# A written order for VectorE and ScalarE around the join of two MLPs

## The chip, the cores and the metric

One core of a Trainium2 chip runs the whole kernel in one launch. The metric is the device time in microseconds. TensorE (PE) multiplies, VectorE (DVE) and ScalarE (ACT) do the elementwise work, SyncE (SP) issues nearly all DMAs, GpSimd is hardly used. Each engine takes its own instructions in their order and waits on semaphores for the others.

## The reference

```python
# q, k, v: (4, 8, 576, 64)
attn = softmax(mask(q @ k.T / sqrt(64))) @ v   # heads 0-3: 32 keys back; heads 4-7: every 32nd key
x = attn.transpose(0, 2, 1, 3).reshape(2304, 512)
h = x @ moe_w_in                     # 512 -> 2048
x = maximum(h, 0)**2 @ moe_w_out     # 2048 -> 512
h = x @ moe2_w_in
out = (h * sigmoid(1.702 * h)) @ moe2_w_out
```

The weights of both MLPs come as 64-bit floats. The kernel's matmuls take 32-bit operands of reduced precision, so each operand is split into a high part and a low remainder, and a product is three matmuls: high by high, low by high, high by low.

## The kernel before

**Weights** are fetched as pairs of 32-bit words and turned into 32-bit floats by five steps (`decode_ops`, lines 138 to 158): ScalarE takes the absolute value of the upper word (L142), VectorE clamps, shifts, and joins the two words (L144, L146, L151, L155). A cast on ScalarE then makes the high part, a subtraction on VectorE the low part.

**The first MLP** runs over five blocks of tokens (512, 512, 256, 512, 512) and, in each, over 16 slices f of the hidden dimension. For a slice TensorE does 12 matmuls into a bank "h" (L412), `act_sq` makes the square and its halves (L441 Relu on ScalarE, L442 high half gh on ScalarE, L443 the square on VectorE, L444 low half gl on VectorE), and while it does so TensorE runs the 12 second-layer matmuls of the slice before (`second`, L469: eight with gh, then four with gl). The attention of later blocks is done beside the earlier ones.

**Preparing the second MLP** happens beside the first MLP's blocks 3 and 4 (counted from 0). `PLAN` (L758) says before which slice what is recorded: "d" converts two slices of the second MLP's first-layer weights (`decode2(0, p)`), forms the seven sums that a Strassen-like scheme needs (L585), splits them into wst (L588, L589) and writes them to w2d in DRAM (L590); "e" converts two slices of its second-layer weights (`decode2(1, p)`, halves whl, L581 and L582); "m" is `make_x`, the sums of the input and their halves xop (L619, L620, L623); "s" streams the products' weights back (L644, L648). Only TensorE's order is the written one here (L727). VectorE's, ScalarE's and SyncE's order is chosen by a scheduler when the program is built, from what is recorded; `issue_after` (L141) keeps a conversion's first step behind a marked instruction of `act_sq`.

**The second MLP** makes three passes over 768 tokens. A pass has two halves of 384 tokens: in the first, eight pairs of slices (f = 2p and 2p + 1) are done as seven products of six matmuls each (`product`, L655) in place of eight; partial results go to X (bank "att"), Y and Z (bank "h"), and are copied and added on ScalarE and VectorE into s1, s2, s3 (L842 to L869). s1 and product 5 give this half's two values per pair, s2 and s3 the other half's, which are kept in gst. Sigmoid and product are `act_sig` (L449, L452), the halves gh and gl `split_g` (L457, L458). Nine second-layer matmuls per slice (`mm_acc2`, L487) follow: six with gh, three with gl. They run one pair later, after products 1 and 4. At the end of the first half the last pair's 18 matmuls are done token tile by token tile with their stores, then the second half does its 16 slices from gst, 9 matmuls each, with `make_x` for the next pass, one operation per slice, between them.

Of the kernel before, what the change touches and what calls it, by code (L numbers as in the profile page):

```python
# [21 lines left out]
def kernel(  # L22
# [88 lines left out]
    marks = [None, None]  # L111
# [26 lines left out]
    def decode_ops(s, t1, mark):  # L138
        low, high = s[:, :, 0], s[:, :, 1]
        ti = t1.bitcast(I32)  # L140
        with tc.issue_after(mark.ins) if mark else ExitStack():  # L141
            nc.scalar.activation(t1, high.bitcast(F32), AF.Abs)  # L142
        yield
# [16 lines left out]
    def decode(n, pool, ntmp):  # L160
# [10 lines left out]
        yield from decode_ops(s.rearrange("p (n two) -> p n two", two=2), t, None)  # L171
# [266 lines left out]
    def act_sq(ph, i):  # L438
        nb = BLOCKS[i][1]
        t, gh, gl = act_tiles(nb)  # L440
        marks[0] = nc.scalar.activation(t, ph[:, 0:nb], AF.Relu)  # L441
        marks[1] = nc.scalar.activation(gh, t, AF.Square)  # L442
        nc.vector.tensor_tensor(out=t, in0=t, in1=t, op=ALU.mult)  # L443
        nc.vector.tensor_tensor(out=gl, in0=t, in1=f32(gh), op=ALU.subtract)  # L444
        return gh, gl

    def act_sig(h, g):
        t, = act_tiles(NH, ("t",))
        marks[0] = nc.scalar.activation(t, h, AF.Sigmoid, scale=1.702)  # L449
        if g is None:  # L450
            g = t
        nc.vector.tensor_tensor(out=g, in0=h, in1=t, op=ALU.mult)  # L452
        return g

    def split_g(g):
        gh, gl = act_tiles(NH, ("gh", "gl"))
        marks[1] = nc.scalar.copy(gh, g)  # L457
        nc.vector.tensor_tensor(out=gl, in0=g, in1=f32(gh), op=ALU.subtract)  # L458
        return gh, gl
# [98 lines left out]
    raw = {}  # L558

    def fetch2(o, p, s):  # L560
        raw[o, p] = s
        for x in range(2):
            fetch_raw(s[:, x], (w2_in, w2_out)[o], 2 * p + x, o)

    def decode2(o, p):
        s, t = raw.pop((o, p)), tmp()
        t2 = t[:, 0:4].rearrange("p (x y) n -> p x (y n)", x=2)
        for x in range(2):
            for _ in decode_ops(s[:, x].bitcast(I32).rearrange("p (n two) -> p n two", two=2), t2[:, x], marks[x]):
                pass  # L570
        if o:
            for x in range(2):
# [3 lines left out]
                elif x == 0:  # L576
                    w2 = slot(f, [2, 2, DM], F32R, "whl")
# [19 lines left out]
    def slot(f, shape, dt, name):  # L597
# [3 lines left out]
        return wpools[n >= NF // 2].tile([P, *shape], dt, tag="w", name=name, bufs=NF // 2 - (FS if n < NF // 2 else 0))  # L601
# [9 lines left out]
    def make_x(s):  # L611
# [5 lines left out]
        def split(j, x):  # L617
            h, l = xops[j][:, 0:2], xops[j][:, 2:4]
            nc.scalar.copy(h, x)  # L619
            nc.vector.tensor_tensor(out=l, in0=x, in1=f32(h), op=ALU.subtract)  # L620

        def sub(out, a, b):
            nc.vector.tensor_tensor(out=out, in0=a, in1=b, op=ALU.subtract)  # L623

        if not wbuf:
            for _ in range(7):
                t_ = slot(0, [2048], F32R, "xop")
                xops.append(t_[:, 0:4 * NH].rearrange("p (h n) -> p h n", h=4))
                wbuf.append(t_[:, 4 * NH:2048].rearrange("p (h n) -> p h n", h=2))
        for fn, args in (  # L630
# [3 lines left out]
            fn(*args)  # L634
            yield
# [92 lines left out]
    stage, xraw = None, None  # L728

    def prepare(what):  # L730

        nonlocal stage, xraw
        for kind, n in what:
            if kind == "stage":
                stage = ring(2, [2, DM], I64, "stage")
            elif kind == "stages":
                stage = ring(1, [2, 2, DM], I64, "stage")
            elif kind in "io":
                fetch2("io".index(kind), n, stage)
            elif kind == "f":  # L740
                fetch2(1, n, stage[:, n % 2])
            elif kind == "d":
                decode2(0, n)
            elif kind == "e":
                decode2(1, n)
            elif kind == "t":

                d = lpool.tile([P, 1], F32, tag="one", name="one", bufs=1)
                nc.scalar.activation(d, f32(gs[4, 0][0][:, 0:1]), AF.Sigmoid)
            elif kind == "x":  # L750
                xraw = load_raw(0, 0)
            elif kind == "m":
                for _ in make_x(xraw):
                    pass
            elif kind == "s":
                stream(n)

    PLAN = {  # L758
# [4 lines left out]
    }  # L763

    for i in range(1, N1):
        for f in range(NF):
# [3 lines left out]
            prepare(PLAN.get((i, f), ()))  # L770
# [26 lines left out]
            gs[i, f] = act_sq(ph, i)  # L797
# [159 lines left out]
```

## Time and profile before

| what | value |
|---|---|
| median of 3 runs (lowest, highest) | 900.73 us (900.62, 901.32) |
| profiled execution, own time | 900.57 us |
| its span, first to last instruction | 898.8 us |
| TensorE busy | 878.7 us, 98% of the span, 5203 matmuls |
| VectorE busy | 553.9 us, 62% |
| ScalarE busy | 447.0 us, 50% |
| granted TensorE clock | 1.00 in all slices |
| DMA, mean rate | 137 GB/s |

The span leaves out some 1.8 us before the first and after the last instruction. Busy shares are means over stages: an engine at 62% can be full for 20 us. Matmuls overlap and their ends are modelled, so the start of one matmul to the start of a later one is what can be measured.

### The profile page before, as it was taken

The numbers are of one execution on the slowest core, as the hardware profiler recorded it, in microseconds if no ns is written. First come the engines' busy times: TensorE is split into PE (matmuls) and PEld (weight loads), VectorE is DVE, ScalarE is ACT, GpSimd is POOL, SyncE is SP. The second block draws the span as 40 slices with busy tenths as digits, with TensorE's granted clock in tenths as the row PEclk, the third lists the DMA queues.
The fourth block names the chain that finished last, engine by engine and source line by source line (L and its number), as shares of the span: only waits on it lengthen the run. The fifth ranks groups of instructions, "written<-read, shape, count | busy, mean of one in ns | idle before, by whom it ended". The sixth has DMA issues, their size and how long they took to land.

```text
span 898.8 us, 14141 instructions
## 1 busy us (share of the span) xinstructions
PE 878.7 (98%) x5203; PEld 749.3 (83%) x5209; DVE 553.9 (62%) x1362; ACT 447.0 (50%) x1153; POOL 2.6 (0%) x12
## 2 busy tenths in 40 slices
PE   8999999999999999999989999999999999999998
PEld 5678887888889998888868899987899978999986
DVE  5999995544546544877797688755344473444432
ACT  7888886453545543445444365543333352333322
POOL 0000000000000000000000000000000000000000
PEclk9999999999999999999999999999999999999999
DMA  8996210221103220556866386553344430344200
GB/s 204 304 334 204 63 27 26 86 53 35 43 20 112 46 71 1 175 202 215 299 233 234 139 276 249 195 184 117 115 163 158 163 129 1 117 164 164 82 36 35
DMA packets 96088, 122.99 MB, mean 137 GB/s; under 512 B 37812, under 2 KB 83604, under 8 KB 93460
## 3 DMA queue, kind: packets, MB, share of 16 engines
q1 hardware_dynamic: 95876, 121.97, 41.5%
q8 instruction: 41, 0.67, 0.3%
q14 instruction: 27, 0.22, 0.1%
q10 hardware_dynamic: 144, 0.13, 0.0%
HBM read 97.96 MB, written 24.12 MB: 136 GB/s over the span
## 4 chain that ended last, share of the span: by engine, by line
PE 79%; DVE 12%; DMA 3%; ACT 3%; issue 2%; SPq 1%; DVEq 0%; ACTq 0%
PE ps_acc L487 21%; PE ps_h L412 17%; PE ps_acc L469 16%; PE ps_att L655 11%; PE ps_h L655 8%; PE ps_att L285 2%; DVE tmp L151 1%; PE ps_h L364 1%; DVE tmp L155 1%; DMA w2d<-wst 1%; PE ps_att L264 1%; PE ps_att L339 1%; DVE whl L181 1%; DVE tmp L144 1%; DVE xop L620 1%
## 5 line engine op out<-in xcount | busy, mean ns | idle before, releaser
L412 PE MATMUL ps_h<-xr,whl 128*128 128x512 f32 (+1 forms) x948 | 211.0, 371 | 0.8 <-DVE whl L181 0.8
L412 PEld LDWEIGHTS ps_h<-xr,whl 128*128 128x128 f32 x948 | 164.4, 188 | 32.0 <-DVE whl L181 1.3
L487 PE MATMUL ps_acc<-whl,gh 128*128 128x512 f32 x576 | 149.1, 392 | 2.6 <-ACT gh L457 2.6
L469 PE MATMUL ps_acc<-gh,whl 128*128 128x512 f32 (+1 forms) x640 | 148.6, 374 | 0.0
L487 PEld LDWEIGHTS ps_acc<-whl,gh 128*128 128x128 f32 x576 | 106.9, 188 | 24.1 <-ACT gh L457 5.1
L469 PEld LDWEIGHTS ps_acc<-gh,whl 128*128 128x128 f32 x640 | 110.3, 188 | 19.1
L315 ACT ACTIVATE pr<-pr,st 72x72 f32<-72x72 f32 (+1 forms) x224 | 81.1, 367 | 20.4 <-DVE st L301 20.4
L441 ACT ACTIVATE t<-ps_h 128x512 f32<-128x512 f32 (+1 forms) x64 | 34.6, 540 | 113.5 <-PE ps_h L412 97.9
L487 PE MATMUL ps_acc<-whl,gl 128*128 128x512 f32 x288 | 82.6, 392 | 2.0 <-DVE gl L458 1.8
L469 PE MATMUL ps_acc<-gl,whl 128*128 128x512 f32 (+1 forms) x320 | 79.0, 369 | 3.7 <-DVE gl L444 3.7
L469 PEld LDWEIGHTS ps_acc<-gl,whl 128*128 128x128 f32 x320 | 56.7, 188 | 14.5 <-DVE gl L444 4.5
L487 PEld LDWEIGHTS ps_acc<-whl,gl 128*128 128x128 f32 x288 | 53.9, 188 | 15.3 <-DVE gl L458 3.8
L443 DVE TENSOR_TENSOR t<-t 128x512 f32<-128x512 f32 (+1 forms) x64 | 39.8, 622 | 34.5 <-ACT gh L442 33.9
L655 PE MATMUL ps_att<-xop 128*128 128x384 f32 x288 | 58.4, 337 | 1.1 <-ACT hs L842 1.1
L449 ACT ACTIVATE t<-hs 128x384 f32<-128x384 f32 x72 | 37.9, 526 | 41.5 <-DVE gst L452 33.5
L655 PE MATMUL ps_att<-xop,wst 128*128 128x384 f32 x288 | 58.5, 338 | 0.0
L655 PEld LDWEIGHTS ps_att<-xop 128*128 128x128 f32 x288 | 51.3, 188 | 3.8 <-ACT hs L842 1.6
L458 DVE TENSOR_TENSOR gl<-gst,gh 128x384 fp32r<-128x384 f32 x45 | 24.8, 556 | 48.1 <-PE ps_acc L487 48.1
L655 PEld LDWEIGHTS ps_att<-xop,wst 128*128 128x128 f32 x288 | 51.6, 187 | 2.0
L457 ACT CAST gh<-gst 128x384 fp32r<-128x384 f32 x45 | 23.1, 515 | 56.1 <-PE ps_acc L487 54.6
L655 PE MATMUL ps_h<-xop,wst 128*128 128x384 f32 x216 | 43.8, 337 | 0.0
L655 PE MATMUL ps_h<-xop 128*128 128x384 f32 x216 | 43.3, 334 | 0.0
(104 smaller groups left out, 1159.0 us busy)
## 6 DMA issues: line engine op xcount, KB each, us to landing
xop<-w2d SPq DMA_DIRECT2D x84, 256.0 KB
wst<-w2d SPq DMA_DIRECT2D x12, 1792.0 KB
w2d<-wst SPq DMA_DIRECT2D x8, 1792.0 KB
stg<-in_moe_w_in_dram SPq DMA_DIRECT2D x16, 512.0 KB
stg<-in_moe_w_out_dram SPq DMA_DIRECT2D x16, 512.0 KB
stage<-in_moe_w_in_dram SPq DMA_DIRECT2D x16, 512.0 KB
stage<-in_moe_w_out_dram SPq DMA_DIRECT2D x16, 512.0 KB
xraw<-x2d SPq DMA_DIRECT2D x3, 1536.0 KB
```

What stands on the lines that cost most here:

```text
L144: nc.vector.tensor_scalar(out=t1, in0=t1, scalar1=EXP_LO, scalar2=EXP_HI, op0=ALU.max, op1=ALU.min)
L285: nc.tensor.matmul(ps[i][0:R, j * P:j * P + N], qT[d, j * R:(j + 1) * R], kT[d, j * N:(j + 1) * N], start=True, stop=True,)
L315: nc.scalar.activation(pr[0:R, i, j, 0:N], pr[0:R, i, j, 0:N], AF.Exp, bias=st[0:R, 0, x:x + 1], scale=-1.0, accum_out=st[0:R, 1, x:x + 1],)
L412: nc.tensor.matmul(ph[:, 0:nb], w[:, kk * P:(kk + 1) * P], x[:, kk], start=(kk == KS[0] and w is ih and x is xh), stop=(kk == KS[-1] and x ...
L441: marks[0] = nc.scalar.activation(t, ph[:, 0:nb], AF.Relu)
L443: nc.vector.tensor_tensor(out=t, in0=t, in1=t, op=ALU.mult)
L449: marks[0] = nc.scalar.activation(t, h, AF.Sigmoid, scale=1.702)
L457: marks[1] = nc.scalar.copy(gh, g)
L458: nc.vector.tensor_tensor(out=gl, in0=g, in1=f32(gh), op=ALU.subtract)
L469: nc.tensor.matmul(acc[c][:, 0:nb], w[:, c * P:(c + 1) * P], x, start=(f == 0 and w is oh and not lo), stop=(f == NF - 1 and lo == 1),)
L487: nc.tensor.matmul(acc[t], x[:, sl], w, start=(f == 0 and w is oh and not lo), stop=(f == NF - 1 and lo == 1),)
L655: nc.tensor.matmul(ps[:, 0:NH], w[:, a, k * P:(k + 1) * P], x[:, b + k], start=start and y == 0, stop=y == len(prods) - 1, skip_group_chec ...
```

## The change

From block 3, slice 5 on, VectorE and ScalarE too keep the order in which the code is written (`manual_schedule` names them; SyncE's order is still chosen). `PLAN` and the marks go. The conversions become one generator that yields after each operation what it costs on "D" (VectorE) or "A" (ScalarE), and `fill(dve, act)` takes operations from it until one of the two rooms is used up: before each block's `act_sq` (3.5, 3.2), twice in a pair of products (2.8, 1.8 and 1.2, 1.2), once per slice of a second half (1.3, 1.3). `fill(99, 99)` empties it. Two more second-layer conversions move ahead of the second MLP, and a second place B for fetched weights lies in a buffer that the first MLP has done with. In `decode2` the two planes are converted one after the other. What is yielded, in us: an Abs 0.66; the four steps of a plane 0.42, 0.42, 0.69, 0.69; for the first layer four sums of 0.43, two casts of 1.04 and 0.82, two subtractions of 1.23 and 0.95 (in all 8.34 on D and 3.18 on A); for the second layer two casts of 0.6 and two subtractions of 0.69 (5.82 and 2.52); in `make_x` seven casts of 0.83 and eleven VectorE operations of 0.95.

From the same slice on, the square t*t is ScalarE's. In a pair, product 2 comes before product 1, the second-layer matmuls of f = 2p come after product 0, and the halves of product 5's value and the work on s2 (`finish`) are written after the next pair's product 0. At the end of a first half, the nine matmuls of f = 14 run before anything of the second half; those of f = 15 follow with the stores, after the halves of f = 0 are written.

```diff
 def act_sq(ph, i):
+        if lpool:
+            nc.scalar.activation(t, t, AF.Square)
+        else:
+            nc.vector.tensor_tensor(out=t, in0=t, in1=t, op=ALU.mult)
...
+    def fill(dve, act):
+        room = {"D": dve, "A": act}
+        while min(room.values()) > 0:
+            did = next(extra, None)
+            if did is None:
+                return
+            room[did[0]] -= did[1]
+
+    def before_mlp2():
+        for p in range(NP):
+            yield from decode2(0, p)
+        for p in range(2):
+            yield from decode2(1, p)
+        yield from make_x(xraw)
+        stream(0)
+        stream(1)
+        for p in range(2, 4):
+            yield from decode2(1, p)
...
 def decode2(o, p):
+        for x in range(2):
+            nc.scalar.activation(t2[:, x], s[x][:, :, 1].bitcast(F32), AF.Abs)
+            yield "A", 0.66
+        for x in range(2):
+            for c, _ in zip((0.42, 0.42, 0.69, 0.69), decode_ops(s[x], t2[:, x], False)):
+                yield "D", c
+        if todo[place]:
+            fetch2(place)
...
             if (i, f) == (3, 5):
+                order.enter_context(tc.manual_schedule(engines={
+                    mybir.EngineType.PE, mybir.EngineType.DVE, mybir.EngineType.Activation}))
+                todo["A"] = [(0, p) for p in range(7)] + [(1, 1), (1, 3)]
+                extra = before_mlp2()
+            if (i, f) == (4, 3):
+                todo["B"] = [(0, 7), (1, 0), (1, 2)]
...
+            if (i, f) >= (3, 6):
+                fill(3.5, 3.2)
             gs[i, f] = act_sq(ph, i)
             second(*prev)
+    fill(99, 99)
...
+    extra = itertools.chain(*(decode2(1, p) for p in range(4, NP)))
...
             product(n, 0, X)
+            finish()
             s1 = hval()
             nc.scalar.copy(s1, X[:, 0:NH])
-            product(n, 1, Z)
-            nc.vector.tensor_tensor(out=s1, in0=Z[:, 0:NH], in1=s1, op=ALU.add)
-            pend[0]()
+            fill(2.8, 1.8)
+            outs[0]()
             product(n, 2, X, start=False)
             s2 = hval()
             nc.scalar.copy(s2, X[:, 0:NH])
-            ga = split_g(act_sig(s1, s1))
+            Z = bank("h")
+            product(n, 1, Z)
+            add(s1, Z)
+            sigmoid(s1, t)
+            times(s1, s1, t)
             product(n, 3, Y)
+            ha = high(s1)
+            ga = low(s1, ha)
             product(n, 4, X, start=False)
             s3 = hval()
             nc.scalar.copy(s3, X[:, 0:NH])
+            add(s3, Y)
+            sigmoid(s3, t)
+            times(gplace(f + 1) if f + 1 < NF - 1 else s3, s3, t)
+            fill(1.2, 1.2)
+            outs[1]()
             product(n, 5, X, start=False)
-            gb = split_g(act_sig(X[:, 0:NH], None))
+            sigmoid(X[:, 0:NH], tx)
+            times(tx, X[:, 0:NH], tx)
             product(n, 6, Y, start=False)
+            def finish(f=f, tx=tx, s2=s2, Y=Y, gb=gb):
+                hb = high(tx)
+                add(s2, Y)
+                gb[0] = low(tx, hb)
+                sigmoid(s2, t)
+                times(gplace(f), s2, t)
...
+        finish()
+        outs[0]()
         for f in range(NF):
+            g = low(g, high(g))
+            if f == 0:
+                for t in T3:
+                    mm_acc2([(NF - 1, gb[0])], acc, [t])
+                    store(i, 0, acc, [t], so)
+            elif f > 1:
+                fill(1.3, 1.3)
```

VectorE in the first MLP's last block, where `make_x` (L620, L623; L647, L651 in the changed kernel) and conversions stand between the low halves gl; before:

```order
L623 TENSOR_TENSOR tmp<-xraw 128x768
L443 TENSOR_TENSOR t<-t 128x512
L151 SCALAR_TENSOR_TENSOR tmp<-stage,tmp 128x512
L146 TENSOR_SCALAR tmp<-tmp 128x512
L623 TENSOR_TENSOR tmp<-xraw,tmp 128x768
L623 TENSOR_TENSOR xraw<-xraw 128x2x384
L444 TENSOR_TENSOR gl<-t,gh 128x512
L155 SCALAR_TENSOR_TENSOR tmp<-stage,tmp 128x512
L151 SCALAR_TENSOR_TENSOR tmp<-stage,tmp 128x512
L620 TENSOR_TENSOR xop<-tmp,xop 128x768 x2
L155 SCALAR_TENSOR_TENSOR tmp<-stage,tmp 128x512
```

and in the changed kernel (L447 is gl, L601 the low part of a second-layer weight):

```order
L447 TENSOR_TENSOR gl<-t,gh 128x512
L601 TENSOR_TENSOR whl<-tmp,whl 128x512
L651 TENSOR_TENSOR tmp<-xraw 128x768
L647 TENSOR_TENSOR xop<-xraw,xop 128x768
L651 TENSOR_TENSOR tmp<-xraw,tmp 128x768
L447 TENSOR_TENSOR gl<-t,gh 128x512
L647 TENSOR_TENSOR xop<-xraw,xop 128x768
L647 TENSOR_TENSOR xop<-tmp,xop 128x768 x2
L651 TENSOR_TENSOR xraw<-xraw 128x2x384
L447 TENSOR_TENSOR gl<-t,gh 128x512
```

The conversions of a first-layer weight no longer stand between the steps of `make_x`, and the square (L443) is gone from this queue; three or four steps stand between two gl.

ScalarE where the second MLP starts (L842 copies product 0 to s1, L848 product 2 to s2, L854 product 4 to s3, L581 is a cast of a converted weight, L142 an Abs); before:

```order
L441 ACTIVATE t<-ps_h 128x512
L442 ACTIVATE gh<-t 128x512
L142 ACTIVATE tmp<-stage 128x512 x2
L581 CAST whl<-tmp 128x512
L842 COPY hs<-ps_att 128x384
L449 ACTIVATE t<-hs 128x384
L848 COPY hs<-ps_att 128x384
L581 CAST whl<-tmp 128x512
L457 CAST gh<-hs 128x384
L854 COPY hs<-ps_att 128x384
```

and in the changed kernel (copies L882, L887, L900; cast L597, Abs L580, sigmoid L451, cast of a half L458):

```order
L441 ACTIVATE t<-ps_h 128x512
L442 ACTIVATE gh<-t 128x512
L444 ACTIVATE t<-t 128x512
L597 CAST whl<-tmp 128x512 x2
L882 COPY hs<-ps_att 128x384
L580 ACTIVATE tmp<-stage 128x512 x2
L887 COPY hs<-ps_att 128x384
L451 ACTIVATE t<-hs 128x384
L458 CAST gh<-hs 128x384
L900 COPY hs<-ps_att 128x384
```

Two casts of the conversion begun in the first MLP, not one, stand in front of s1's copy, and the next conversion's two Abs come behind it. VectorE there, in the changed kernel, from the first MLP's last gl to the add of s1 (L864):

```order
L447 TENSOR_TENSOR gl<-t,gh 128x512
L155 SCALAR_TENSOR_TENSOR tmp<-stage,tmp 128x512
L144 TENSOR_SCALAR tmp<-tmp 128x512
L146 TENSOR_SCALAR tmp<-tmp 128x512
L151 SCALAR_TENSOR_TENSOR tmp<-stage,tmp 128x512
L155 SCALAR_TENSOR_TENSOR tmp<-stage,tmp 128x512
L601 TENSOR_TENSOR whl<-tmp,whl 128x512 x2
L144 TENSOR_SCALAR tmp<-tmp 128x512
L146 TENSOR_SCALAR tmp<-tmp 128x512
L151 SCALAR_TENSOR_TENSOR tmp<-stage,tmp 128x512
L155 SCALAR_TENSOR_TENSOR tmp<-stage,tmp 128x512
L144 TENSOR_SCALAR tmp<-tmp 128x512
```

Thirteen conversion steps (the last is one more L146) now stand between that gl and the add; before, eight stood there and both planes were interleaved.

ScalarE between the halves of a pass, from the sigmoid of product 5's value on (L619 and L645 are casts of `make_x`, L819 and L856 copies for a store); before:

```order
L449 ACTIVATE t<-ps_att 128x384
L619 CAST xop<-xraw 128x768
L457 CAST gh<-t 128x384
L449 ACTIVATE t<-hs 128x384
L819 COPY tmp<-ps_acc 128x512
L619 CAST xop<-tmp 128x768
L457 CAST gh<-gst 128x384
```

and in the changed kernel:

```order
L451 ACTIVATE tx<-ps_att 128x384
L458 CAST gh<-tx 128x384
L451 ACTIVATE t<-hs 128x384
L458 CAST gh<-gst 128x384
L856 COPY tmp<-ps_acc 128x512
L458 CAST gh<-gst 128x384 x2
L645 CAST xop<-xraw 128x768
```

The cast of product 5's value follows its sigmoid at once, and the casts of f = 0, 1 and 2 stand in front of the first cast of `make_x`.

## Rows read from the trace of the kernel before

**Rows 1.** Waits of TensorE after 330 us: total, times, longest (us).

```profile
PE ps_acc L469 <- DVE gl L444: 3.7, 2, 2.6
```

**Rows 2.** Windows: busy PE, PEld, DVE, ACT, POOL; clock, DMA share, GB/s.

```profile
450.00:470.00 20.00, 16.30 (x72) 12.83 (x70) 19.29 (x32) 7.87 (x13) 0.00 (x0) 1.00 0.74 255
470.00:506.00 36.00, 36.00 (x159) 29.82 (x160) 24.36 (x41) 16.35 (x26) 0.00 (x0) 1.00 0.39 147
```

**Rows 3.** Timeline, 415 to 475 us: start, length, instruction, wait before it.

```profile
458.52 2.00 PE L469 MATMUL ps_acc<-gh,whl 128*128 128x512 f32 x8
...
460.66 0.95 DVE L623 TENSOR_TENSOR tmp<-xraw,tmp 128x768 f32<-128x768 f32 x1
...
462.40 0.68 DVE L444 TENSOR_TENSOR gl<-t,gh 128x512 fp32r<-128x512 f32 x1
...
463.14 1.20 PE L469 MATMUL ps_acc<-gl,whl 128*128 128x512 f32 x4 [2.61 <-DVE gl L444]
...
466.90 1.97 PE L469 MATMUL ps_acc<-gh,whl 128*128 128x512 f32 x8
...
469.96 1.20 PE L469 MATMUL ps_acc<-gl,whl 128*128 128x512 f32 x4 [1.08 <-DVE gl L444]
```

**Rows 4.** Timeline, 475 to 530 us, TensorE in an undisturbed block.

```profile
479.15 1.98 PE L469 MATMUL ps_acc<-gh,whl 128*128 128x512 f32 x8
...
480.97 1.07 PE L469 MATMUL ps_acc<-gl,whl 128*128 128x512 f32 x4
```

**Rows 5.** The same timeline at the start of the second MLP.

```profile
506.36 1.98 PE L469 MATMUL ps_acc<-gh,whl 128*128 128x512 f32 x8
506.55 0.60 ACT L441 ACTIVATE t<-ps_h 128x512 f32<-128x512 f32 x1 [4.18 <-PE ps_h L412]
...
511.18 2.01 PE L469 MATMUL ps_acc<-gh,whl 128*128 128x512 f32 x8
...
513.81 0.47 ACT L842 COPY hs<-ps_att 128x384 f32<-128x384 f32 x1
...
514.34 1.31 PE L655 MATMUL ps_att<-xop 128*128 128x384 f32 x6 [1.14 <-ACT hs L842]
```

**Rows 6.** Timeline of TensorE between the halves of the first pass.

```profile
600.12 1.21 PE L655 MATMUL ps_h<-xop,wst 128*128 128x384 f32 x6
601.17 0.63 PE L487 MATMUL ps_acc<-whl,gh 128*128 128x512 f32 x2
...
610.63 1.54 PE L487 MATMUL ps_acc<-whl,gh 128*128 128x512 f32 x6
...
612.70 1.53 PE L487 MATMUL ps_acc<-whl,gh 128*128 128x512 f32 x6
```

**Rows 7.** The same in the third pass.

```profile
857.40 0.63 PE L487 MATMUL ps_acc<-whl,gh 128*128 128x512 f32 x2
...
864.38 1.53 PE L487 MATMUL ps_acc<-whl,gh 128*128 128x512 f32 x6
```

**Rows 8.** Groups by line and shape; count, busy us, mean ns, idle before.

```profile
L449 ACT ACTIVATE t<-hs 128x384 f32<-128x384 f32 x72 | 37.9, 526 | 41.5 <-DVE gst L452 33.5 <-DVE hs L844 3.6 <-DVE gl L458 2.8
...
L442 ACT ACTIVATE gh<-t 128x512 fp32r<-128x512 f32 x48 | 30.3, 632 | 1.0
...
L452 DVE TENSOR_TENSOR gst<-hs,t 128x384 f32<-128x384 f32 x45 | 24.9, 554 | 8.9 <-ACT t L449 8.9
...
L151 DVE SCALAR_TENSOR_TENSOR tmp<-stage,tmp 128x512 int32<-128x512 int32 x32 | 22.0, 687 | 0.3
...
L142 ACT ACTIVATE tmp<-stage 128x512 f32<-128x512 f32 x32 | 21.1, 664 | 3.7 <-DMA stage<-in_moe_w_out_dram 3.0 <-DMA stage<-in_moe_w_in_dram 0.7
...
L146 DVE TENSOR_SCALAR tmp<-tmp 128x512 int32<-128x512 int32 x36 | 15.3, 424 | 0.6
```

**Rows 9.** Timeline, 415 to 475 us: a write of wst, and who waited.

```profile
429.68 0.60 SPq L590 DMA_DIRECT2D w2d<-wst  x1
...
441.74 1.78 ACT L588 CAST wst<-tmp 128x1024 fp32r<-128x1024 f32 x2 [3.53 <-DMA w2d<-wst]
```

More of the change, by code (lines that the diff above doesn't have):

```diff
@@ L170, in decode @@
         s = s.bitcast(I32).rearrange("p o x -> p (o x)") if both else s.bitcast(I32)
-        yield from decode_ops(s.rearrange("p (n two) -> p n two", two=2), t, None)
+        yield from decode_ops(s.rearrange("p (n two) -> p n two", two=2), t)
         w = wtile(f, o, [2, DM], F32R, "whl")
@@ L440, in act_sq, with sigmoid, times, high @@
         t, gh, gl = act_tiles(nb)
-        marks[0] = nc.scalar.activation(t, ph[:, 0:nb], AF.Relu)
-        marks[1] = nc.scalar.activation(gh, t, AF.Square)
-        nc.vector.tensor_tensor(out=t, in0=t, in1=t, op=ALU.mult)
+        nc.scalar.activation(t, ph[:, 0:nb], AF.Relu)
+        nc.scalar.activation(gh, t, AF.Square)
+        if lpool:
+            nc.scalar.activation(t, t, AF.Square)
+        else:
+            nc.vector.tensor_tensor(out=t, in0=t, in1=t, op=ALU.mult)
         nc.vector.tensor_tensor(out=gl, in0=t, in1=f32(gh), op=ALU.subtract)
         return gh, gl
[L447 to L451, printed above, removed]
-        nc.vector.tensor_tensor(out=g, in0=h, in1=t, op=ALU.mult)
[L453 to L457, printed above, removed]
+    def sigmoid(h, t):
+        nc.scalar.activation(t, h, AF.Sigmoid, scale=1.702)
+    def times(g, h, t):
+        nc.vector.tensor_tensor(out=g, in0=h, in1=t, op=ALU.mult)
+    def high(g):
+        gh, = act_tiles(NH, ("gh",))
+        nc.scalar.copy(gh, g)
+        return gh
+    def low(g, gh):
+        gl, = act_tiles(NH, ("gl",))
         nc.vector.tensor_tensor(out=gl, in0=g, in1=f32(gh), op=ALU.subtract)
@@ L633, in make_x @@
         ):
-            fn(*args)
-            yield
+            yield from fn(*args)
     wbuf, wcur = [], {}
@@ L727 @@
     order.enter_context(tc.manual_schedule(engines={mybir.EngineType.PE}))
[L728 to L758, printed above, removed]
[4 rows of a table removed]
-    }
+    extra = iter(())
+    def fill(dve, act):
[15 more added lines that the diff above has]
+            yield from decode2(1, p)
     for i in range(1, N1):
@@ L874 @@
                 acc = [bank("acc") for _ in T3]
-            def outs(f, g, acc=acc):
-                return lambda: mm_acc2([(f, g)], acc, T3)
-            pend = [outs(f, ga), outs(f + 1, gb)]
-        so = stores()
-        for t in T3:
-            mm_acc2([(f, ga), (f + 1, gb)], acc, [t])
-            store(i, 0, acc, [t], so)
-        steps = make_x(xraw) if i + 1 < N2 else iter(())
-        acc = [bank("acc") for _ in T3]
-        held = []
-        for f in range(NF):
-            g = split_g(gplace(f) if f < NF - 1 else s3)
-            if f > 1:
-                next(steps, None)
+            gb = [None]
@@ L891 @@
+        acc2, held = None, []
+        for f in range(NF):
+            g = gplace(f) if f < NF - 1 else s3
+            g = low(g, high(g))
+            if f == 0:
+                so = stores()
+                for t in T3:
+                    mm_acc2([(NF - 1, gb[0])], acc, [t])
+                    store(i, 0, acc, [t], so)
+                acc2 = [bank("acc") for _ in T3]
+            elif f > 1:
+                fill(1.3, 1.3)
             held.append((f, g))
             if f < NF - 2:
-                mm_acc2(held, acc, T3)
+                mm_acc2(held, acc2, T3)
@@ L894, with end @@
                 held = []
+        so = stores()
         if i + 1 < N2:
-            so = stores()
-            def end(i=i, acc=acc, held=held, so=so):
+            fill(99, 99)
+            finish = nothing
+            def end(i=i, acc=acc2, held=held, so=so):
                 mm_acc2(held[1:], acc, T3)
                 store(i, 1, acc, T3, so)
-            pend = [lambda acc=acc, held=held: mm_acc2(held[:1], acc, T3), end]
+            outs = [lambda acc=acc2, held=held: mm_acc2(held[:1], acc, T3), end]
```

116 lines of the change are left out of this document (69 added, 47 removed), and 4 rows, old and new, of the table PLAN.

## Prediction

> **What bounds the kernel now.** The table of the profile section says it first: TensorE is busy for 878.7 of 898.8 us, so the end moves only where TensorE stands still, and the views to read are those that show its gaps. I read the waits of TensorE for the changed part (after 330 us) first: the longest is for VectorE's low half gl in the first MLP, 3.7 us in two times [rows 1]. Then the windows: VectorE is busy for 19.29 of 20 us from 450 to 470, and there TensorE does 16.30 us; from 470 to 506 VectorE has room and TensorE does 36.00 of 36 [rows 2]. So VectorE is no bound on average (62% in the table) but is one in that stretch. Last the timeline, where I measure each gap from start to start, since ends of matmuls are modelled.
>
> There are three kinds of gap. *In the last block row of the first MLP*, eight matmuls with a high half go over into four with a low half in 1.82 us where nothing is late (479.15 to 480.97) [rows 4]; at 458.52 and 466.90 it takes 4.62 and 3.06 us, because the subtraction for gl began only at 462.40, behind operations for the second MLP such as the 0.95 us one at 460.66 [rows 3]. Lost: 2.80 + 1.24 = 4.04 us. *At the start of the second MLP* the eight matmuls of 511.18 reach the next product at 514.34, after the ScalarE copy of s1 at 513.81 [rows 5]: 3.16 - 1.82 = 1.34 us. *Between the halves of a pass* 27 matmuls (18 for the last two f, 9 for f = 0) run from 601.17 to 610.63, 9.46 us; nine run from 610.63 to 612.70, 2.07 us [rows 6], so 27 cost 6.21 and 3.25 us are lost. The second pass does the same to 0.01 us, the third (857.40 to 864.38) loses 6.98 - 6.21 = 0.77 [rows 7]. Together 7.27 us. The rest of the changed part is matmul after matmul.
>
> **The change, part by part.** *The queue in the first MLP.* No matmul is added or dropped. Before each block's own ScalarE and VectorE work some 3.5 to 4.2 us of conversions are now written on VectorE, so at most one such portion stands in front of a gl. Does it fit? A block is 24 matmuls, 24 x 1.82 / 8 = 5.46 us [rows 4]. The code's cost numbers are borne out by the rows (0.66 against 664 ns, 0.42 against 424, 0.69 against 687) [rows 8]. By them VectorE's queue is eight first-layer conversions of 8.34, two second-layer ones of 5.82, make_x 10.45 and two more of 5.82: 100.4 us, of which 4.3 are left over after the last block. The other 96.1 over 26 blocks are 3.70, with gl 4.39 us of 5.46. ScalarE's part is 8 x 3.18, 3 x 2.52, 5.81 for make_x and two Abs more, 40.1 us, 1.54 a block, with Relu and now two squares 1.86 more: 3.40 of 5.46. A block's Relu starts 0.19 us after its matmuls [rows 5]; gh is done 0.60 + 0.63 later and needed after the 5.46 us of the other matmuls: 4.0 us of room. I take all 4.04 us as gained. The bounds are 0 (the stalls only move) and 4.04.
>
> *The square t*t* goes from VectorE (0.69) to ScalarE (0.63 [rows 8]); both sides lie under the sums just made, so it costs nothing; without that cover the low half is a fraction of a microsecond earlier or later, against room of over 4 us.
>
> *The halves of a pass.* After the last product TensorE now runs the nine matmuls of f = 14 first (2.07 us), whose halves have long been there. Those of f = 15 need, from the end of product 5, a sigmoid 0.53, a product 0.55, a cast like a sigmoid 0.53, a subtraction 0.55 [rows 8]: 2.16, and about 0.3 for the handing over; product 6 (1.05 [rows 6]) covers the first part and f = 14 the rest, 3.12 against 2.5. The first operation for the next x, which stood in front of these in both queues, now comes at f = 2 and later, 1.3 us at a time. I take all 7.27; bounds 0 and 7.27.
>
> *The pairs.* The products now run 0, f, 2, 1, 3, 4, f, 5, 6: the same matmuls and the same number of turns between kinds, so I give the steady pair the same length. What could be late is s3's copy, now behind s1's whole chain on ScalarE: add 0.55, sigmoid 0.53, product 0.55, cast 0.53, copy 0.47, 2.63 and some 0.4 of handing over, against two products and nine matmuls, 2 x 1.05 + 2.07 = 4.17. Room 1.1 us, so 0; the upper bound is what the first pair loses below, in each of the five further pairs that hold conversions: 5 x 1.24 = 6.2 us.
>
> *The start of the second MLP gets worse.* Times from the end of the last block's first-layer matmuls (506.36 before). In the written order VectorE does gl, then what is left of the conversion of f = 6 and 7, one plane after the other; ScalarE has that conversion's second cast in front of s1's copy.
> - First wait: Relu 0.19 + 0.60, two squares 0.63 each: 2.05. VectorE: 0.69 (gl), 0.69, 0.42, 0.42, 0.69, 0.69: 5.65. Cast 0.63, copy 0.47: 6.75. TensorE stands before product 2 at 12 matmuls 2.73 + product 1.05 + eight 1.82 = 5.60. Lost 1.15.
> - Second: behind s1's copy come the Abs of the next conversion (0.66) and six VectorE operations 0.42, 0.42, 0.69, 0.69, 0.42, 0.42 in front of s1's add: 10.47; then the 2.63 of the chain above to s3's copy: 13.10. TensorE stands before product 5 at 6.75 + 4 x 1.05 + 0.91 = 11.86. Lost 1.24.
> - Third: from 13.10 s3's add, sigmoid and product 1.63, two conversion steps 1.38, two spills of the first MLP's sums 1.38 (taken as the 687 ns row), then product 0.55, cast 0.53, sigmoid 0.53, copy 0.47: 19.57. TensorE is there at 13.10 + 3 x 1.05 + 2.07 = 18.32. Lost 1.25.
>
> That is 3.64 where 1.34 were: 2.30 us more. Bounds: 0 (the queue is ahead of this sum) and double, 7.3.
>
> **The sum** against the profiled execution's own time, 900.57 us: 900.57 - 4.04 - 7.27 + 2.30 = 891.56. The median of the runs, 900.73, is 0.16 above that execution, so **891.7 us**.
>
> **The rivals.** *Slower: the written order makes ScalarE stand for a transfer with Relu behind it.* In the queue two casts into wst or two Abs of freshly fetched weights stand in front of each Relu. One write of wst took from its issue at 429.68 to the cast that waited for it at 441.74, 12.06 us [rows 9], next to other transfers; the scheduler had put nothing urgent behind that cast. A fetch is issued about 3.9 us of VectorE's queue (one block, 5.7 us) before its Abs; if fetches took 12.06 us, ScalarE would stand 6.3 us, 2.3 over the room of 4.0. With eight of the twelve conversions: 891.6 + 18.6 + 0.2, 910 us; it is slower than before from the fourth on. For it: blocks 1 to 5 of the last row, where x2 is spilled and read back beside the writes. Against it: only this one wait of ScalarE on wst stands in the trace, and it is the sum of several transfers. What VectorE did at 462.40 is the same thing in small: operations that nobody needed yet held the one that TensorE stood for [rows 3]. The Trainium skill says in "PSUM — Partial Sum Buffer", Engine vs sequencer instructions, that "ScalarE/VectorE/GpSimdE queues are strict FIFO". By that rule a written order can't let Relu pass, and it speaks against the change wherever a wait in the queue is longer than the room; at 462.40 the trace agrees with it, 2.61 us of TensorE.
>
> *No change: the first pair's backlog is not caught up.* If in each of the five further pairs with conversions one of s3's and s1's copies is late as in the first, it is 5 x 1.24 = 6.2 more, 897.9; if both are, 5 x 2.49 = 12.5, 904.2. In the middle, 901, nothing is gained. For it: room of only 1.1 us; against it: VectorE has 9 x 0.55 + 4 = 9 us of work in a pair of 11.5, so that a backlog shrinks.
>
> *Half a gain: the turn between the halves keeps half its loss*, because the stores of three sums still stand in both queues between the casts for f = 0 and f = 1: 891.7 + 3.6 = 895.3.
>
> *More: the start costs nothing*, if VectorE arrives with less left over: 891.7 - 3.6 = 888.1.
>
> **How the numbers follow.** Forecast 0.52 (its own range 889.5 to 894.5), half a gain 0.15, the cheap start 0.10, no change 0.10, slower 0.13. A measurement of this kernel tells 0.2%, 1.8 us, from no change: faster means below 898.9, slower above 902.5. The first three cases are faster (0.77); no change is spread over 898 to 904 and falls mostly within, with a little on either side; so faster 0.78, same 0.08, slower 0.14. The range for 8 in 10 reaches from 888 (the cheap start) to 900.5 (half of the case of no change).
>
> **What would show it.** Right: the waits of TensorE for gl in the first MLP are gone, and VectorE's windows there are even, about 4.4 us in 5.46; 27 matmuls between the halves take 6.2 to 6.5 us in all three passes; three waits of about 1.2 us each stand in the first 20 us of the second MLP, on the copies of s1, s3 and s1. Wrong: ScalarE waits on transfers in front of Relu with TensorE idle behind it; waits on s3's copy in pair after pair; or no wait at all at the start.

## The result, and the profile after

The changed kernel takes 891.14 us (median of 4 runs, 890.79 to 892.48) against 901.03 us in the same session (900.62 to 901.66): a ratio of 0.9892, 95% interval 0.9875 to 0.991. 891.7 was predicted. The profiled execution took 890.83 us, its span is 889.0.

The page's row of engines (busy us, share, instructions) and the waits of TensorE after 330 us (total, times, longest) are, in the changed kernel:

```profile
PE 876.3 (99%) x5203; PEld 750.3 (84%) x5209; DVE 544.8 (61%) x1335; ACT 464.9 (52%) x1180; POOL 2.6 (0%) x12
```

```profile
PE ps_att L683 <- ACT hs L882: 1.8, 2, 1.1
...
PE ps_att L683 <- ACT hs L900: 1.0, 1, 1.0
...
PE ps_acc L474 <- ACT gh L442: 0.5, 1, 0.5
```

The wait for gl [rows 1] is gone, and so are those for gh and gl between the halves, which before were

```profile
PE ps_acc L487 <- ACT gh L457: 2.6, 5, 0.7
PE ps_acc L487 <- DVE gl L458: 1.8, 2, 0.9
```

Three waits at the start of the second MLP and a small new one, on gh, are what is left. The windows that answer to [rows 2] (busy PE, PEld, DVE, ACT, POOL; clock, DMA share, GB/s) show VectorE even where it was full before, 17.10 us in 20 and 27.56 in 36, and TensorE without a gap in both (the first row is for the new wait, below):

```profile
431.00:453.00 22.00, 21.46 (x95) 17.47 (x94) 14.00 (x25) 12.77 (x20) 0.00 (x0) 1.00 0.97 361
450.00:470.00 20.00, 20.00 (x90) 16.57 (x89) 17.10 (x31) 13.14 (x22) 0.00 (x0) 1.00 0.76 280
470.00:506.00 36.00, 36.00 (x162) 30.00 (x161) 27.56 (x43) 22.87 (x37) 0.00 (x0) 1.00 0.43 159
```

The new wait, in the timeline of the changed kernel (start, length, instruction, wait before it):

```profile
435.72 1.98 PE L474 MATMUL ps_acc<-gh,whl 128*128 128x512 f32 x8
...
440.00 0.66 ACT L580 ACTIVATE tmp<-stage 128x512 f32<-128x512 f32 x1 [4.43 <-DMA stage<-in_moe_w_in_dram]
440.57 0.58 ACT L441 ACTIVATE t<-ps_h 128x512 f32<-128x512 f32 x1
...
441.86 2.11 PE L474 MATMUL ps_acc<-gh,whl 128*128 128x512 f32 x8 [0.54 <-ACT gh L442]
```

That is the slower rival in small: ScalarE stands 4.43 us for fetched weights, in a stretch where the DMA share is 0.97 (431 to 453), with a Relu behind it. The Relu's input was ready at about 435.9; it starts at 440.57, 4.66 us late, against a room of 4.0. From one slice's first-layer matmuls to the next's (438.44 to 444.71) the block takes 6.27 us in place of 5.44, 0.83 lost. It happened once. By the rule of the Trainium skill that the prediction names ("PSUM — Partial Sum Buffer", Engine vs sequencer instructions) nothing may pass the waiting instruction, and here nothing did.

The start of the second MLP answers to [rows 5]:

```profile
501.83 1.98 PE L474 MATMUL ps_acc<-gh,whl 128*128 128x512 f32 x8
...
505.62 2.01 PE L474 MATMUL ps_acc<-gh,whl 128*128 128x512 f32 x8
...
508.16 0.47 ACT L882 COPY hs<-ps_att 128x384 f32<-128x384 f32 x1
...
508.68 1.34 PE L683 MATMUL ps_att<-xop 128*128 128x384 f32 x6 [1.05 <-ACT hs L882]
...
512.98 1.08 PE L474 MATMUL ps_acc<-gl,whl 128*128 128x512 f32 x4
...
515.02 1.33 PE L683 MATMUL ps_att<-xop 128*128 128x384 f32 x6 [0.96 <-ACT hs L900]
...
518.29 1.55 PE L492 MATMUL ps_acc<-whl,gh 128*128 128x512 f32 x6
...
521.29 1.33 PE L683 MATMUL ps_att<-xop,wst 128*128 128x384 f32 x6 [0.76 <-ACT hs L882]
```

From start to start (eight matmuls take 1.82 us, four 0.91, nine 2.07) the three waits lose 3.06 - 1.82 = 1.24, 1.13 and 0.93 us: 3.30. Between the halves of the first pass, which answers to [rows 6], nine matmuls of f = 14 run from 598.90, nine of f = 15 tile by tile from 600.98, and nine of f = 0 from 603.02 to 605.06:

```profile
598.90 1.55 PE L492 MATMUL ps_acc<-whl,gh 128*128 128x512 f32 x6
...
600.98 0.62 PE L492 MATMUL ps_acc<-whl,gh 128*128 128x512 f32 x2
...
603.02 1.52 PE L492 MATMUL ps_acc<-whl,gh 128*128 128x512 f32 x6
...
605.06 1.52 PE L492 MATMUL ps_acc<-whl,gh 128*128 128x512 f32 x6
```

6.16 us for 27, where it was 9.46; the second pass takes 6.16 and the third 6.17.

**Where the time went.** The part of the program that is the same in both differs from one execution to the next: the matmuls of block 3, slice 5, where the change begins, start at 357.88 before and at 356.84 after, and in the runs below anywhere up to 361.30. (The two above 360 are the profiled executions of e8 and e10, 892.61 and 901.25 us, which lie above these kernels' medians; in both TensorE's clock fell there, see the last section.) So I compare two stretches of each profiled execution that don't hold it: from there to the matmuls of the last block (26 blocks of 5.44 us, 141.44 when nothing is late; what is over is lost), and from these to the start of the last row of TensorE's timeline.

| kernel | median us | ratio to before, 95% | lost in 26 blocks | rest |
|---|---|---|---|---|
| before | 900.86 to 901.13 | 1 | 4.31 | 390.90 |
| changed | 891.14 | 0.9892 (0.9875 to 0.991) | 0.83 | 385.67 |
| e1 no backlog | 888.74 | 0.9855 (0.9833 to 0.9877) | 1.94 | 382.08 |
| e2 pairs in old order | 891.85 | 0.9883 (0.9863 to 0.9904) | 0.93 | 386.07 |
| e3 old turn | 893.45 | 0.9906 (0.9886 to 0.9925) | 1.09 | 387.67 |
| e4 t*t on VectorE | 894.83 | 0.9925 (0.9907 to 0.9944) | 1.53 | 388.12 |
| e5 first MLP's order free | 887.82 | 0.9854 (0.9841 to 0.9867) | 0.02 | 383.28 |
| e6 second MLP's order free | 889.38 | 0.9873 (0.986 to 0.9886) | 0.91 | 384.06 |
| e7 late fetch | 890.99 | 0.9892 (0.9879 to 0.9905) | 0.80 | 385.62 |
| e8 light start | 888.59 | 0.987 (0.9854 to 0.9887) | 0.90 | 382.90 |
| e9 e5 with t*t on VectorE | 891.67 | 0.9904 (0.9889 to 0.9919) | 3.93 | 383.22 |
| e10 before with t*t on ScalarE | 897.87 | 0.9973 (0.9961 to 0.9985) | 1.60 | 391.03 |
| e11 e6 with the old turn | 895.98 | 0.9953 (0.9936 to 0.9971) | 0.84 | 390.13 |
| e12 e5, light start | 886.42 | 0.9846 (0.9829 to 0.9862) | 0.02 | 382.08 |

### The profile page after: what moved, and what is told of

It reads as the page before. It is cut to its first block, busy times and chain, and to the rows that moved or that the text cites. A ratio compares the mean times of both kernels' runs of the same rounds, so it can differ in the third digit from the quotient of the medians.

```text
span 889.0 us, 14124 instructions
## 1 busy us (share of the span) xinstructions
PE 876.3 (99%) x5203; PEld 750.3 (84%) x5209; DVE 544.8 (61%) x1335; ACT 464.9 (52%) x1180; POOL 2.6 (0%) x12
## 4 chain that ended last, share of the span: by engine, by line
PE 82%; DVE 7%; DMA 5%; ACT 3%; issue 1%; SPq 1%; ACTq 0%; DVEq 0%
PE ps_acc L492 22%; PE ps_acc L474 18%; PE ps_h L412 18%; PE ps_att L683 11%; PE ps_h L683 8%; DMA stg<-in_moe_w_in_dram 2%; DMA stg<-in_moe_w_out_dram 2%; PE ps_att L285 2%; PE ps_h L364 1%; DVE tmp L155 1%; DVE tmp L151 1%; PE ps_att L339 1%; DMA stage<-in_moe_w_in_dram 1%; PE ps_att L264 1%; DVE whl L181 1%
## 5 line engine op out<-in xcount | busy, mean ns | idle before, releaser
L864 DVE TENSOR_TENSOR hs<-ps_h,hs 128x384 f32<-128x384 f32 x72 | 40.0, 555 | 68.1 <-PE ps_h L683 68.1
L451 ACT ACTIVATE t<-hs 128x384 f32<-128x384 f32 x72 | 37.9, 526 | 49.1 <-DVE hs L864 47.7
L447 DVE TENSOR_TENSOR gl<-t,gh 128x512 fp32r<-128x512 f32 (+1 forms) x64 | 40.0, 625 | 31.7 <-ACT t L444 30.1
L458 ACT CAST gh<-gst 128x384 fp32r<-128x384 f32 x45 | 23.2, 516 | 44.8 <-PE ps_acc L492 44.5
L315 ACT ACTIVATION_READ_ACCUMULATOR pr<-pr,st 72x1 f32 (+1 forms) x224 | 44.2, 197 | 0.0
```

The source lines that it names most:

```text
L315: nc.scalar.activation(pr[0:R, i, j, 0:N], pr[0:R, i, j, 0:N], AF.Exp, bias=st[0:R, 0, x:x + 1], scale=-1.0, accum_out=st[0:R, 1, x:x + 1],)
L864: nc.vector.tensor_tensor(out=h, in0=ps[:, 0:NH], in1=h, op=ALU.add)
```

## Experiments

**e1: nothing left over at the start.**

```
-  fill(3.5, 3.2)
+  room = (3.5, 3.2) if (i, f) < (4, 6) else (4.2, 3.8)
+  fill(*room)
   ...
-  fill(2.8, 1.8)   # and fill(1.2, 1.2)
+  if n > 0: fill(2.8, 1.8)
```

> The changed kernel, but the queue's room is 4.2 and 3.8 us a block from block 4, slice 6 on (it was 3.5 and 3.2), and the first pair of the second MLP takes nothing from the queue. My theory: what TensorE lost at the start of the second MLP (3.30 us in three waits: 1.24 on s1's copy, 1.13 on s3's copy, 0.93 on the next s1's copy) is the queue's leftover standing ahead of those copies. Then all three waits go and the time falls by 3.0 to 3.3 us, to about 888.0. Rival: the leftover only moves. VectorE would have about 5.0 of 5.44 us a block full in the last ten blocks, gl comes late again, 0.2 to 0.3 us a block, and little is left: 890 to 891.5.

888.74 us. All three waits at the start are gone, so the leftover was their cause; but 1.1 us of it comes back in the last blocks, as the rival said, though through another engine:

```profile
495.44 0.62 ACT L597 CAST whl<-tmp 128x512 fp32r<-128x512 f32 x1 [1.63 <-DVE tmp L155]
495.96 0.60 ACT L441 ACTIVATE t<-ps_h 128x512 f32<-128x512 f32 x1
...
497.28 2.12 PE L474 MATMUL ps_acc<-gh,whl 128*128 128x512 f32 x8 [0.29 <-ACT gh L442]
```

A cast of the queue waits for VectorE, and Relu, gh and TensorE wait behind the cast. It is gh that comes late, not gl.

**e2: the old order of products 0, 1, 2.** `Z = bank("h"); product(n, 1, Z)` goes back ahead of `outs[0]()`.

> The changed kernel with products 0, 1 and then 2 of a pair in the old order (1 ahead of the queued matmuls again). My theory: in the steady pairs the order has no price and no gain (11.51 us either way), but s1's copy gets the 1.05 us of product 1 more as room, so that of the start's waits the two on s1's copies (1.24 and 0.93) nearly go: 2.0 us less, 889.1. Rival A: the wait only moves to s3's copy, no change, 891.1. Rival B: the new order is what lets VectorE and ScalarE keep up in a pair, and without it every one of the 24 pairs has a wait of 0.2 to 0.3 us: 896 to 898.

891.85 us; the intervals of this and the changed kernel overlap. The wait moved, as rival A says: 0.21 us on s1's copy and none on the next, but 2.20 on s3's. That is 2.41 us where the changed kernel has 3.30; but behind the long wait TensorE's clock falls and costs some 1.5 us (last section), so the equal times don't show that the reordering is worth nothing at the start. In the later pairs, which have no wait in either order, it is.

**e3: the old turn between the halves, order still held.**

```
-  outs[0]()
+  so = stores()
+  for t in T3:
+      mm_acc2([(NF - 2, ga), (NF - 1, gb[0])], acc, [t])
+      store(i, 0, acc, [t], so)
```

(and the same loop taken out of f = 0.)

> The changed kernel with the turn between the halves of a pass as before: the last two slices tile by tile, the stores' copies, and only then the first slice of the second half. My theory: the turn was worth what the prediction says, so the loss comes back: 27 matmuls take 9.4 us in two passes and 7.0 in the third in place of 6.16, +6.5 to +7.3 us, about 898. Rival: the written order already keeps the copies and casts in the right places, so the turn alone is worth under 1 us a pass: +1 to +3, 892 to 894.

893.45 us: the rest is 2.0 us longer, the rival's number. The timeline of the first turn:

```profile
599.75 0.63 PE L492 MATMUL ps_acc<-whl,gh 128*128 128x512 f32 x2
...
600.58 0.73 PE L492 MATMUL ps_acc<-whl,gh 128*128 128x512 f32 x2 [0.21 <-ACT gh L458]
...
604.35 1.54 PE L492 MATMUL ps_acc<-whl,gh 128*128 128x512 f32 x6
...
606.55 1.55 PE L492 MATMUL ps_acc<-whl,gh 128*128 128x512 f32 x6
```

27 matmuls take 6.80 us, 0.64 more than in the changed kernel and 2.66 less than before. So the turn alone isn't what was worth 7.3 us.

**e4: t*t on VectorE, order held.** `if lpool: nc.scalar.activation(t, t, AF.Square)` goes, and VectorE's product stands for all blocks.

> The changed kernel with the square t*t on VectorE again in all blocks. My theory (the move is worth nothing): VectorE has 4.4 of 5.44 us a block full and takes 0.7 more, ScalarE loses 0.63; gl comes no later than the next block needs it, 890.8 to 891.6. Rival: VectorE is then so full (5.1 of 5.44) that where the queue overshoots its room by an operation of 0.95 to 1.23 us gl comes late: 0.2 to 0.4 us in 10 of 26 blocks, 893 to 895.

894.83 us: the rival's size at another place. After 330 us the list of TensorE's waits is

```profile
PE ps_att L681 <- ACT hs L880: 3.9, 2, 3.3
PE ps_acc L471 <- ACT gh L442: 0.8, 1, 0.8
```

No wait on gl returns: the held order keeps gl in time with t*t on VectorE too. The blocks lose 1.53 us, 1.09 of them at the fetch that costs 0.83 in the changed kernel, and 0.42 on another gh. But VectorE arrives later at the start (the last gl begins 4.58 us after the last block's first-layer matmuls, not 2.22), where s1's copy now costs 3.59 us, and TensorE's clock falls there (last section). My "worth nothing" was wrong.

**e5 and e6: the order of VectorE and ScalarE not held in the first, or in the second MLP.** e5 leaves out `manual_schedule` for them until `fill(99, 99)`, e6 after it; TensorE keeps its order.

> The changed kernel with the same code for the first MLP's last blocks (queue of pieces, t*t on ScalarE), but the order of VectorE and ScalarE is held only from the second MLP on; before that the scheduler sets it, as in the kernel before. My theory: the held order is what keeps gl in its place, so TensorE's waits on gl come back, 2.5 to 4 us: 893.5 to 895. Rival: the cutting into pieces and t*t on ScalarE are enough, and the order that is written adds nothing: 890.5 to 891.7.

> The changed kernel with the order of VectorE and ScalarE held in the first MLP only; in the second MLP the code is as in the changed kernel (products, turn between the halves, queue), but the scheduler sets the order on these two engines. My theory, after the old turn under a held order gave back only 2.0 of 7.3 us: the other 5 us come from the order, because the scheduler moves the operations that prepare the next pass ahead of the casts and subtractions that TensorE waits for. So the turns of the first two passes lose 2 to 2.7 us each again and the third little: 895 to 897. Rival: with the turn rewritten TensorE has cover for them (18 matmuls, 4.1 us), so the order adds nothing there: 890.5 to 892.

887.82 and 889.38 us: both faster than the changed kernel, and both of my theories fell. e5 has no wait in the 26 blocks and one at the start. The windows show how; the first fence is the changed kernel, the second e5:

```profile
453.00:485.00 32.00, 32.00 (x143) 26.50 (x142) 26.62 (x44) 20.22 (x32) 0.00 (x0) 1.00 0.80 293
485.00:501.00 16.00, 16.00 (x72) 13.23 (x72) 12.54 (x19) 10.54 (x18) 0.00 (x0) 1.00 0.00 0
```

```profile
453.00:485.00 32.00, 32.00 (x143) 26.50 (x142) 32.00 (x55) 22.90 (x38) 0.00 (x0) 1.00 0.63 229
485.00:501.00 16.00, 16.00 (x73) 13.23 (x72) 3.88 (x6) 6.73 (x11) 0.00 (x0) 1.00 0.00 0
```

The scheduler works VectorE full, 32.00 of 32 us, without TensorE noticing, and has only gl left from 490 us on; the held order doles out 3.5 us a block and carries the remainder into the start. There, e5's timeline has s1's copy 0.20 us after the next matmuls begin, not 2.54:

```profile
505.21 2.01 PE L474 MATMUL ps_acc<-gh,whl 128*128 128x512 f32 x8
...
505.41 0.48 ACT L878 COPY hs<-ps_att 128x384 f32<-128x384 f32 x1 [1.86 <-PE ps_att L683]
...
507.06 1.23 PE L683 MATMUL ps_att<-xop 128*128 128x384 f32 x6
```

In e6 the turns take the same 6.16 us; its gain of 1.6 us in the rest is at the start, where two waits of 0.80 and 0.69 us from start to start, on s3's add in front of product 6, take the place of three.

**e7: the fetch written later.** `fetch2(place)` moves from behind a place's last read to the end of `decode2`.

> The changed kernel with each fetch of the next weights issued at the end of a conversion (behind its last operation) in place of right behind its last read of the place. It tests the rival on the slow side: ScalarE standing for a transfer with the Relu behind it. My theory: in the held order that rival is real and has only been kept off by the fetch's lead (from 376.94 to 385.03 us, 8.1 us, in one conversion). With no lead ScalarE waits 2 to 4 us at each of 8 to 10 conversions, of which some 2 us are TensorE's slack; 0.5 to 2 us reach TensorE each time: 896 to 908. Rival: the lead doesn't matter, as ScalarE comes to these reads late anyway: 890.5 to 892.

890.99 us, but it tells nothing: the order on SyncE, which the scheduler sets, came out the same, so no fetch was issued later. What a shorter lead would cost stays open; the one wait at 440.00 is all there is on it. As a repeat of the changed kernel it agrees to 0.15 us.

**e8: one conversion moved into the second MLP.** `before_mlp2` ends with pair 2, `fill(3.4, 2.4)` and `fill(1.2, 1.2)` in all pairs but the first, with five conversions there and a `fill(99, 99)` behind the last pair.

> The changed kernel with one conversion (second layer, pair 3) moved out of the first MLP's queue into the second's, the first pair of the second MLP taking nothing from the queue, and the later pairs with a room of 3.4 and 2.4 in place of 2.8 and 1.8. My theory: nothing is left over when the second MLP starts, so its three waits (3.30 us) go, and without the fuller blocks that cost 1.1 us in the run with more room (a cast of the queue held ScalarE's Relu up at 495.96 us): 887.7 to 888.2. Rival: the five conversions don't fit into seven pairs, and s1's or s3's copies wait there, 0.3 to 0.5 us a pair: 889.5 to 891.

888.59 us, 2.7 us less than the changed kernel in the two stretches: the waits at the start go, one of 0.24 us at 529.08 is left, and the first MLP loses no more than it did. Its median is above what I expected by 0.4, within its runs' spread (887.8 to 892.61).

**e9 and e10: what ended the waits on gl.** e9 is e5 with t*t back on VectorE; e10 is the kernel before with

```
-  nc.vector.tensor_tensor(out=t, in0=t, in1=t, op=ALU.mult)
+  if lpool:
+      nc.scalar.activation(t, t, AF.Square)
+  else:
+      nc.vector.tensor_tensor(out=t, in0=t, in1=t, op=ALU.mult)
```

> The kernel of e5 (the first MLP's order left to the scheduler, 887.82 us) with t*t on VectorE again. It is one corner of a square: pieces or whole conversions in the code, t*t on ScalarE or on VectorE, all under the scheduler's order. Theory A: the move of t*t is what ended TensorE's waits on gl, as gl no longer needs two turns on a VectorE that the conversions fill; then the waits of the kernel before return, 3 to 4 us: 890.8 to 892. Theory B: the queue's pieces, written between the blocks, ended them; then nothing changes: 887.3 to 888.5.

> The kernel before with one edit: t*t on ScalarE (a second Square in place) from block 3, slice 5 on. The opposite corner of the square: whole conversions, scheduler's order, t*t on ScalarE. Theory A (the move ended the waits on gl): 3 to 4 us less than before, 897 to 898. Theory B (the pieces did): the waits on gl of 2.6 and 1.1 us stay, 900 to 902.

891.67 and 897.87 us: theory A in both corners. 26 blocks lose:

| | t*t on VectorE | t*t on ScalarE |
|---|---|---|
| whole conversions, scheduler's order | 4.31 (before) | 1.60 (e10) |
| pieces, scheduler's order | 3.93 (e9) | 0.02 (e5) |
| pieces, held order | 1.53 (e4) | 0.83 (changed) |

(The code with pieces also does two more conversions in these blocks.) Under the scheduler's order the move takes away 2.7 us by itself and 3.9 with the pieces; the pieces by themselves 0.4. In the third row no wait on gl is left in either column, so the held order with the pieces ends these waits as well; most or all of what it loses, 1.09 and 0.83 us, is the wait for fetched weights. The timeline of e9 shows how gl comes late under the scheduler's order:

```profile
476.11 0.70 DVE L443 TENSOR_TENSOR t<-t 128x512 f32<-128x512 f32 x1
476.71 0.96 DVE L648 TENSOR_TENSOR tmp<-xraw,tmp 128x768 f32<-128x768 f32 x1
477.58 1.30 DVE L151 SCALAR_TENSOR_TENSOR tmp<-stage,tmp 128x512 int32<-128x512 int32 x2
...
478.79 0.69 DVE L444 TENSOR_TENSOR gl<-t,gh 128x512 fp32r<-128x512 f32 x1
...
479.54 1.19 PE L471 MATMUL ps_acc<-gl,whl 128*128 128x512 f32 x4 [1.47 <-DVE gl L444]
```

gh is done at 474.54. t*t and gl are two turns on a full VectorE, with foreign operations ahead of each: 4.94 us from gh to the end of gl. VectorE is as full in e5, 32.00 of 32 us from 453 to 485 in both, and there no gl is late. Whether the turn that is saved does it or the 0.69 us of work, the runs don't part. In e10 one wait is left, its only one on gl in the first MLP:

```profile
PE ps_acc L472 <- DVE gl L447: 1.3, 1, 1.3
```

**e11: old turn, order free.** e3's edit in e6.

> The kernel of e6 (second MLP's order left to the scheduler, 889.38 us) with the old turn between the halves. The last corner of a square: old turn under a held order lost 0.64 us a turn, new turn under a free order nothing. My theory: either one gives the cover, and only both missing lose what the kernel before lost, 3.25, 3.25 and 0.8 us: 895.5 to 897. Rival: the casts and subtractions of the next pass now come in smaller pieces, which by itself keeps them out of the way: +1 to +2.5, 890.3 to 892.

895.98 us; the rest is 6.1 us longer than e6's. My theory holds for the first two passes (for the third see the next section). The rest of the four corners:

| | old turn | new turn |
|---|---|---|
| order free | 390.13 (e11) | 384.06 (e6) |
| order held | 387.67 (e3) | 385.67 (changed) |

(The held row holds the dearer start as well, 1.6 us.) The timeline of the first turn in e11:

```profile
596.87 0.63 PE L492 MATMUL ps_acc<-whl,gh 128*128 128x512 f32 x2
596.89 0.83 ACT L645 CAST xop<-xraw 128x768 fp32r<-128x768 f32 x1 [0.38 <-PE ps_h L683]
...
598.19 0.73 PE L492 MATMUL ps_acc<-whl,gh 128*128 128x512 f32 x2 [0.70 <-ACT gh L458]
...
602.94 1.66 PE L492 MATMUL ps_acc<-whl,gh 128*128 128x512 f32 x6 [0.46 <-ACT gh L458]
...
605.19 0.98 PE L492 MATMUL ps_acc<-whl,gl 128*128 128x512 f32 x3 [0.59 <-DVE gl L463]
...
606.01 1.55 PE L492 MATMUL ps_acc<-whl,gh 128*128 128x512 f32 x6
```

A cast for the next x stands ahead of gh, and the stalls of [rows 6] are back: 27 matmuls take 9.14 us. In e6 the same cast stands there, and the nine matmuls of f = 14 cover it.

**e12: the best of it.** e5 with `if n > 0` ahead of both fills of a pair.

> The kernel of e5 (first MLP's order left to the scheduler, 887.82 us) with nothing taken from the queue in the first pair of the second MLP. My theory: its last wait of TensorE after block 3 (on s1's copy at 518.55 us, 0.78 on the page, 0.93 in the matmuls' spacing) stands behind that pair's conversion on VectorE and goes: 886.8 to 887.0, and there is then no wait left from 376 us to the end. Rival: the conversions come one pair later and the wait moves to a later pair: 887.5 to 888.2.

886.42 us, 0.9846 of before (0.9829 to 0.9862), the fastest kernel here, and 4.7 us below the changed one. After 330 us its list of TensorE's waits is empty.

## Why the prediction came out right, and what in it was wrong

The time was right to 0.6 us; the two stretches give -8.71 us where the sum said -9.01, and the other microsecond is the difference ahead of the change. That the sum comes so near is partly luck: its terms miss by 0.56 us to one side (the queue) and by 0.14 and 0.34 us to the other (the halves, the start).

- **The queue in the first MLP, -4.04: size near, one of two causes seen.** The blocks lost 4.31 and lose 0.83, so -3.48: all waits on gl went, and one on gh came. VectorE's share was right (43.83 us in 55, 4.33 a block, against 4.39). I gave the gain to the order and the queue, and they are enough for it: with t*t back on VectorE (e4) no gl is late. But the move of t*t, priced at nothing, does it too: e5 has no wait with the order free, and e10 has 2.7 us of the gain with neither queue nor held order. The held order without the queue was not run.
- **t*t "costs nothing": the step that failed.** I compared sums per block, and by those both engines have room. Under the scheduler's order that is not what decides: in e9 the chain has to get past foreign work on a full VectorE twice, and the move is worth 2.7 to 3.9 us. Under the held order it is worth 3.2 (531.1 against 527.9 us from the change's start to TensorE's last row, e4), though gl is in time either way, as I had said: 0.7 in the blocks, 1.1 in waits at the start, because VectorE comes there later, and some 1.5 by TensorE's clock.
- **The halves, -7.27: size right, cause half right.** 27 matmuls take 6.16 us, against 6.21, in all three passes: 3.30, 3.30 and 0.81 us. The prediction gave two reasons as one, cover by f = 14 and the next x standing further back. The corners part them: in the first two passes either one does most of it (the order leaves 0.64 us a turn, the cover nothing), and they don't add. In the third only the cover does: with the old turn 27 matmuls take 6.81 us under the held order (e3) and 6.65 under the free one (e11), against 6.98 before.
- **Pairs, 0: right.** 11.51 us, no wait after the third.
- **The start, +2.30: right, measured +1.96.** Three waits on the copies of s1, s3 and s1, of 1.24, 1.13 and 0.93 us where I had 1.15, 1.24 and 1.25. The causes are as worked out (e1, e8). What I didn't see is that this is the price of the order held in the first MLP with a fixed room per block, and not of the other edits: with the order free the conversions are done before the start, and one wait of 0.93 us is left (e5).
- **The rivals.** The slower one exists and happened once, 0.83 us: the transfer that ScalarE stood for overran the room of 4.0 us by 0.7, not by 2.3 eight times. The half gain didn't come (6.16 us a turn), and no backlog reached a later pair. The cheap start is what e1, e5, e8 and e12 make.

## What to carry to other kernels

Where a short chain of a bottleneck's inputs runs through an engine that is filled with preparing work, count how many times it must queue there, and move steps to an engine with room: in the first MLP's blocks this took away 3.9 us (e9 to e5), the written order 2.4 (e9 to e4). A written order protects such a chain, but it also fixes how much preparing work each block does, and what it leaves over is paid where the next stage begins; try it against the scheduler's order, stage by stage. Where two edits each remove the same wait, the gains don't add, so a run of one alone says little: run all four corners.

## What was not expected of the hardware

After a wait TensorE sometimes ran at half speed for a while. In e4, TensorE's timeline and a window of it:

```profile
512.37 1.38 PE L681 MATMUL ps_att<-xop 128*128 128x384 f32 x6 [3.30 <-ACT hs L880]
513.55 3.78 PE L681 MATMUL ps_h<-xop 128*128 128x384 f32 x12
```

```profile
513.55:517.10 3.55, 3.55 (x13) 3.55 (x13) 2.88 (x6) 1.00 (x2) 0.00 (x0) 0.53 0.45 144
```

Twelve matmuls take 3.62 us from start to start, where 2.12 are usual: the granted clock is 0.53 in the window (0.50, the lower level of 1.2 GHz, up to 516 us), after a stand of 3.30 us. In e2 it is 0.50 for 2 us after a wait of 2.02 us (the weight loads stood 2.45). After 2.61 us before the change [rows 3] it stayed at 1.00. Nor did the wait have to be long. In the part of the program that all runs share, e8 shows

```profile
59.74 0.44 PE L264 MATMUL ps_att<-ident,ld 72*128 72x72 f32 x4 [1.15 <-DMA ld<-in_q_dram]
60.51 0.44 PE L264 MATMUL ps_att<-ident,ld 72*128 72x72 f32 x4 [0.33 <-DVE tmp L155]
60.75 3.27 PE L474 MATMUL ps_acc<-gh,whl 128*128 128x512 f32 x8
```

and the clock is 0.50 from 62 to 64 us; eight matmuls reach the next four at 63.82, in 3.07 us and not 1.82. In e10 it is 0.50 from 38 to 44 us, behind a wait of 1.08 us for a fetch of q. In the changed kernel it is 1.00 in that whole part. What tells these cases apart the runs don't show; where the clock fell at the start of the second MLP (e2, e4), it cost some 1.5 us that no list of waits has.
